# Four x loads on two queues, a split wq, q before k, more dummy matmuls, and wo last: a change to the start and the end of a TensorE-bound attention and feed-forward kernel

## The chip, the cores and the metric

The kernel runs on one core of one Trainium2 chip. The metric is the device time of one execution in microseconds (us). A profiled execution gives a trace; its span, from the first to the last instruction, is 1.5 to 1.8 us shorter than that time.

Engine names are those of the profile: PE is TensorE's matmuls and PEld its weight loads, DVE is VectorE, ACT ScalarE, POOL GpSimd. SP only issues DMA loads and stores; ACT issues some as well ("SPq", "ACTq").

## The reference, cut to what matters

```python
x = A_x                                            # [1, 2048, 512], bf16
g = sigmoid((x * gate_w).sum(-1, keepdims=True))
a = A_ref(x, wq, wk, wv, wo, beta)                 # 32 heads of 16, four segments of 512 tokens
b = B_ref(x, W_gate, W_up, W_down)                 # (relu(x Wg) * (x Wu)) Wd, width 1792
return g * a + (1 - g) * b

# in A_ref, per segment s:
#   a_dot = causal softmax attention within the segment
#   a_mem = phi(q) M / (phi(q) z)                  # memory of the earlier segments
#   o     = sigmoid(beta) * a_mem + (1 - sigmoid(beta)) * a_dot,  then M, z are updated
# the result of A_ref is o @ wo
```

`beta` is 32 numbers, 64 bytes.

Of the kernel before, what the change touches and what calls it, by code (L numbers as in the profile page):

```python
# [18 lines left out]
def mm(n, k=1):  # L19
    return k * (max(n, 60) / 2.4 + 2.5)  # L20
# [359 lines left out]
def program(sc, nc, T, PL, PA, A_x, A_wq, A_wk, A_wv, A_wo, A_beta, W_g, W_u, W_d, gate_w, out, NSEG, KT, NF, NT, EPS, SCALE):  # L380
    V = type("V", (), T)
# [30 lines left out]
    def load(eng, names, dst, src, nbytes, occ=460.0):  # L412
        (lact if eng == "act" else lsp).append(dma(eng, lambda e, dst=dst, src=src: e.dma_start(dst, src), nbytes, occ=occ, writes=names, name="ld" + names[0]))
    x0 = A_x[0, 0:512, :].rearrange("(i p) d -> p i d", p=128)
    for i in (0, 2):
        load("sp", [f"hT{i}", f"hT{i + 1}"], V.hT[:, i:i + 2, :], x0[:, i:i + 2, :], 1 << 18)
    for nm, w, src in (("wq", V.wq, A_wq), ("wk", V.wk, A_wk), ("wv", V.wv, A_wv)):
        load("sp", [nm], w[:], src.rearrange("(kt p) n -> p kt n", p=128), 1 << 19)
    wgr = W_g.rearrange("(kt p) n -> p kt n", p=128)
    wur = W_u.rearrange("(kt p) n -> p kt n", p=128)  # L420
    half = (NF // 2) * 128
# [7 lines left out]
    def load_x(c):  # L429
        for kt in range(KT):  # L430
            lsp.append(dma("sp", lambda e, c=c, kt=kt: e.dma_start_transpose(V.xT[:, kt, c * 512:(c + 1) * 512], A_x[0, c * 512:(c + 1) * 512, kt * 128:(kt + 1) * 128]),
                           1 << 17, occ=1280.0, writes=[f"xT{c}_{kt}"], name=f"ldx{c}_{kt}"))
    load("act", ["braw"], V.braw[:], A_beta.partition_broadcast(128), 8192)
    load_gu(0)
    gsrc = gate_w.rearrange("(kt p) -> p kt", p=128)

# [50 lines left out]
            return ins  # L487
        return pe(fn, n * 427, reads=["rl0"], writes=[f"bankL{b}"], name=f"warm{k}")

    xps, xcs = [warm(5, 0, 3)], []  # L490
    for i in range(4):
        def fx(e, i=i):
            for kt in range(KT):
# [3 lines left out]
        for h in range(2):  # L497
# [3 lines left out]
                xcs.append(dve(lambda e, d=dst, s_=srcp: e.tensor_copy(d, s_), t_dve(256), reads=[f"bankL{i}"], writes=[f"xT0_{i}a"], name=f"xc{i}"))  # L501
            else:
                xcs.append(act(lambda e, d=dst, s_=srcp: e.activation(d, s_, ACT.Copy), t_act(256), reads=[f"bankL{i}"], writes=[f"xT0_{i}b"], name=f"xc{i}"))
    xps.append(warm(2, 1, 0))
    sc.queue(0, xps)
    sc.queue(0, [t for t in xcs if t.eng == "dve"])
    sc.queue(0, [t for t in xcs if t.eng == "act"])
# [49 lines left out]
    def proj(s):  # L557
        pes, evs, sbs, acts, sps = [], [], [], [], []
        tok = s * 512

        def pj(w, col, name, wname, tokmajor=False):
            ep = Epoch("proj")

            for k0 in range(0, KT, 2):
                def fn(e, k0=k0):
                    for kt in (k0, k0 + 1):
                        if tokmajor:
                            ins = e.matmul(A(ep)[:, :], lhsT=V.xT[:, kt, tok + col * 128:tok + (col + 1) * 128], rhs=w[:, kt, :], start=(kt == 0), stop=(kt == KT - 1))  # L568
                        else:
                            ins = e.matmul(A(ep)[:, :], lhsT=w[:, kt, col * 128:(col + 1) * 128], rhs=V.xT[:, kt, tok:tok + 512], start=(kt == 0), stop=(kt == KT - 1))  # L570
                    return ins
                pes.append(pe(fn, mm(512, 2), reads=[wname] + xt(s), name=f"{name}{s}_{col}", ep=ep, role="w2" if k0 else "w"))
            return ep
        for G in range(4):
            ep = pj(V.wq, G, "q", "wq")
            qs = qslot(s, G)
            evs.append(dve(lambda e, ep=ep, qs=qs: e.tensor_copy(V.qT[:, qs, :], A(ep)[:, :]), t_dve(512), writes=[f"qT{qs}"], name=f"qcp{s}_{G}", ep=ep, role="r"))
            if s > 0:
                acts.append(act(lambda e, qs=qs, G=G: e.activation(V.phiq[:, G, :], V.qT[:, qs, :], ACT.Exp), t_act(512, False), reads=[f"qT{qs}"], writes=[f"phiq{G}"], name=f"qexp{s}_{G}"))
                sbs.append(dve(lambda e, qs=qs, G=G: e.tensor_scalar(V.ttmp[:, G % 2, :], V.qT[:, qs, :], 0.0, 1.0, ALU.max, ALU.add), t_dve(512, 4), reads=[f"qT{qs}"], writes=[f"ttmp{G % 2}"], name=f"qts{s}_{G}"))  # L580
                sbs.append(dve(lambda e, G=G: e.tensor_tensor(V.phiq[:, G, :], V.phiq[:, G, :], V.ttmp[:, G % 2, :], ALU.min), t_dve(512, 2), reads=[f"phiq{G}", f"ttmp{G % 2}"], writes=[f"phiq{G}"], name=f"qphi{s}_{G}"))
            ep = pj(V.wk, G, "k", "wk")
            evs.append(dve(lambda e, ep=ep, G=G: e.tensor_copy(V.kT[:, G, :], A(ep)[:, :]), t_dve(512), writes=[f"kT{G}"], name=f"kcp{s}_{G}", ep=ep, role="r"))
            for p in range(2):
                ks = kslot(s, 2 * G + p)
                evs.append(dve(lambda e, G=G, p=p, ks=ks: e.tensor_scalar(V.kp[:, ks, :], V.kT[:, G, :], V.pm[:, p:p + 1], None, ALU.mult), 417, reads=[f"kT{G}", "pm"], writes=[f"kp{ks}"], name=f"kmask{s}_{G}_{p}"))
            if s < NSEG - 1:
                acts.append(act(lambda e, G=G: e.activation(V.ek[:, G, :], V.kT[:, G, :], ACT.Exp), t_act(512, False), reads=[f"kT{G}"], writes=[f"ek{G}"], name=f"kexp{s}_{G}"))
                sbs.append(dve(lambda e, G=G: e.tensor_scalar(V.ttmp[:, G % 2, :], V.kT[:, G, :], 0.0, 1.0, ALU.max, ALU.add), t_dve(512, 4), reads=[f"kT{G}"], writes=[f"ttmp{G % 2}"], name=f"kts{s}_{G}"))
                sbs.append(dve(lambda e, G=G: e.tensor_tensor(V.ek[:, G, :], V.ek[:, G, :], V.ttmp[:, G % 2, :], ALU.min), t_dve(512, 2), reads=[f"ek{G}", f"ttmp{G % 2}"], writes=[f"ek{G}"], name=f"kphi{s}_{G}"))  # L590
                sps.append(dma("sp", lambda e, G=G: e.dma_start_transpose(V.phik[:, :, G * 128:(G + 1) * 128], V.ek[:, G, :]), 1 << 17, occ=1280.0, reads=[f"ek{G}"], writes=[f"phik{G}"], name=f"kT2{s}_{G}"))
        for tt in range(4):
            ep = pj(V.wv, tt, "v", "wv", True)
            evs.append(dve(lambda e, ep=ep, tt=tt: e.tensor_copy(V.vaug[:, s % 2, tt, :, 0:16], A(ep)[:, :].rearrange("q (h c) -> q h c", c=16)), t_dve(512), writes=[f"va{s % 2}_{tt}"], name=f"vcp{s}_{tt}", ep=ep, role="r"))
        return pes, evs, sbs, acts, sps

    def va(s):
# [149 lines left out]
    def outp(s, slots):  # L747
        tiles, evs, sps = [], [], []
        o0 = (s % 2) * 4
        for i in range(4):  # L750
            t = 4 * s + i
            for c0, c1 in (((0, 512),) if t < NT - 1 else ((0, 256), (256, 512))):
                pes = []
                ep = Epoch("out")
                w = c1 - c0

                def fa(e, i=i, ep=ep, c0=c0, c1=c1):
                    for G in range(4):
                        ins = e.matmul(A(ep)[:, 0:c1 - c0], lhsT=V.oT[:, o0 + G, i * 128:(i + 1) * 128], rhs=V.wo[:, G, c0:c1], start=(G == 0), stop=False)  # L759
                    return ins  # L760
                need = slots if s < NSEG - 1 else slots[:NF - 4]
                pes.append(pe(fa, mm(w, 4), reads=[f"oT{o0 + G}" for G in range(4)] + ["wo", "wd"] + [f"hT{x}" for x in need], name=f"oa{s}_{i}", ep=ep, role="w"))
                for f0 in range(0, NF, 2):
                    fs = list(range(f0, min(f0 + 2, NF)))

                    def fb(e, i=i, ep=ep, fs=fs, c0=c0, c1=c1):
                        for f in fs:
                            ins = e.matmul(A(ep)[:, 0:c1 - c0], lhsT=V.hT[:, slots[f], i * 128:(i + 1) * 128], rhs=V.wd[:, f, c0:c1], start=False, stop=(f == NF - 1))  # L768
                        return ins
                    pes.append(pe(fb, mm(w, len(fs)), reads=[f"hT{slots[f]}" for f in fs] + ["wd"], name=f"ob{s}_{i}_{f0}", ep=ep, role="w2"))  # L770
                tiles.append(pes)
                r = t % 3
                om = V.omg[:, t:t + 1]
                res = [f"osb{r}_0", f"osb{r}_1"] if w == 512 else [f"osb{r}_{c0 // 256}"]
                evs.append(sc.add(Op([("dve", lambda e, ep=ep, r=r, om=om, c0=c0, c1=c1: e.tensor_scalar(V.osb[:, r, c0:c1], A(ep)[:, 0:c1 - c0], om, None, ALU.mult), t_dve(w)),  # L775
                                      ("act", lambda e, ep=ep, r=r, om=om, c0=c0, c1=c1: e.activation(V.osb[:, r, c0:c1], A(ep)[:, 0:c1 - c0], ACT.Copy, scale=om), t_act(w, True, 1))],  # L776
                                     reads=[f"omg{min(s, 1)}"], writes=res, name=f"fin{s}_{i}", ep=ep, role="r")))
                sps.append(dma("sp", lambda e, r=r, t=t, c0=c0, c1=c1: e.dma_start(out[0, t * 128:(t + 1) * 128, c0:c1], V.osb[:, r, c0:c1]), w * 256,
                               reads=res, writes=[f"out{t}_{c0}"], name=f"st{t}"))
        if s == NSEG - 1:  # L780
            tiles = [tiles[0][:-1] + tiles[1][:-1] + tiles[0][-1:] + tiles[1][-1:]] + tiles[2:]
        return [p for g in tiles for p in g], evs, sps

    Q = {k: [] for k in ("patt", "pnd", "pmu", "pproj", "pffn", "pout", "exp", "aphi", "dproj", "dsb", "datt", "dnd", "dmu", "effn", "eout", "pool", "poolmu", "spk", "spa", "spo")}
# [32 lines left out]
    sc.queue(1, Q["datt"])  # L817
    for px in ("qcp", "kcp", "vcp"):
        sc.queue(0, [t for t in Q["dproj"] if t.name.startswith(px)])
    sc.queue(1, [t for t in Q["dproj"] if t.name.startswith("kmask")])  # L820
    sc.queue(1, Q["effn"])
    sc.queue(1, Q["eout"])
    sc.queue(1, Q["dnd"])
# [48 lines left out]
```

## The kernel before: the parts that the change and the argument touch

A small list scheduler orders all operations at build time with its own cost model, assigns PSUM banks (where TensorE's results go) and semaphores (counters that tell an engine that something it waits for is done), and emits one program for each engine. So moving one load can reorder the whole program. The loads at the start are these:

```python
x0 = A_x[0, 0:512, :].rearrange("(i p) d -> p i d", p=128)
for i in (0, 2):                                   # two loads of 256 KB, on SP
    load("sp", [f"hT{i}", f"hT{i + 1}"], V.hT[:, i:i + 2, :], x0[:, i:i + 2, :], 1 << 18)
for nm, w, src in (("wq", V.wq, A_wq), ("wk", V.wk, A_wk), ("wv", V.wv, A_wv)):
    load("sp", [nm], w[:], src.rearrange("(kt p) n -> p kt n", p=128), 1 << 19)
# ... cut ...
load("act", ["braw"], V.braw[:], A_beta.partition_broadcast(128), 8192)   # beta to all 128 partitions
load_gu(0)                                         # first halves of W_gate and W_up, on SP
```

The first 512 tokens of x are transposed on TensorE, with dummy matmuls around them that only keep TensorE busy:

```python
xps, xcs = [warm(5, 0, 3)], []                     # five dummy matmuls of 512 columns
for i in range(4):                                 # four 128 x 128 transposes for each x tile
    # ... fx: e.matmul(PL[:, i, ...], lhsT=V.hT[:, i, ...], rhs=V.ident[:]) ...
    # then half of each tile is copied to xT by DVE, the other half by ACT
xps.append(warm(2, 1, 0))                          # two dummies, then the q projections
```

In each segment the projections go q, k, q, k, and so on, then v. In each output tile the four `wo` products come first and 14 `W_down` products follow; the last segment's tiles end the program.

The softmax here doesn't subtract the row's maximum and nothing guards it: scores larger than these inputs give would overflow.

## Time and profile before

| | before |
|---|---|
| time, median of the 6 runs beside the changed kernel | 277.94 us (277.82 to 278.92) |
| span of the profiled execution | 276.13 us |
| PE busy | 269.6 us (98%) |
| first transpose of x | 5.71 us |
| wq landed (issue 1.83 + 6.07) | 7.90 us |
| first weight load of the q projections | 8.54 us |
| end of the last weight load | 273.31 us |

From the page of the profile: span, busy times of the engines, and the chain that ended last, by engine.

```profile
span 276.1 us, 5357 instructions
...
PE 269.6 (98%) x2201; PEld 116.8 (42%) x2201; DVE 196.6 (71%) x390; ACT 193.4 (70%) x171; POOL 91.7 (33%) x152
...
PE 94%; DMA 2%; ACT 2%; DVE 1%; issue 0%
```

TensorE is the limit. A change can help only by starting its stream of useful matmuls sooner, by making that stream shorter, or by ending sooner after it. The start is in the timeline (start, duration, engine, line and operation, count, and in brackets the idle time before it and what ended it):

```profile
0.80 0.42 ACTq L413 DMA_DIRECT2D braw<-in_A_beta_dram  x1
0.80 0.97 SPq L413 DMA_DIRECT2D hT<-in_A_x_dram  x2
...
1.25 2.31 PE L486 MATMUL psL<-rl 128*128 128x512 bf16 x5 [1.25 <-DVE rl L477]
...
5.71 1.89 PE L494 MATMUL psL<-ident,hT 128*128 128x128 bf16 x16 [2.15 <-DMA hT<-in_A_x_dram]
...
7.39 1.06 PE L486 MATMUL psL<-rl 128*128 128x512 bf16 x2
...
8.54 0.13 PEld L570 LDWEIGHTS psA<-xT,wq 128*128 128x128 bf16 x2 [1.00 <-ACT xT L503]
8.55 1.54 PE L570 MATMUL psA<-xT,wq 128*128 128x512 bf16 x4
```

TensorE idles 2.15 us until x lands. The five dummies start 0.43 us apart, twice the 0.215 us that 512-column matmuls take later: the clock is halved. It is still halved for the first q matmuls. The first five matmuls of the projections start at 8.55, 8.95, 9.37, 9.70 and 9.92 us, 1.37 us for four steps that take 0.86 us at the full clock, so 0.51 us of useful work is lost to the clock.

The view of windows gives busy times of PE, PEld, DVE, ACT and POOL in each stretch, then the granted clock (not reliable before the first clock record, as here), the DMA share and the DMA rate in GB/s:

```profile
2.50:3.25 0.75, 0.75 (x3) 0.15 (x1) 0.70 (x2) 0.03 (x1) 0.61 (x3) 1.00 0.50 101
3.25:4.00 0.75, 0.32 (x1) 0.00 (x0) 0.22 (x2) 0.00 (x0) 0.68 (x3) 1.00 0.75 197
...
5.50:6.25 0.75, 0.54 (x6) 0.54 (x7) 0.66 (x6) 0.00 (x0) 0.00 (x0) 1.00 1.03 367
```

The rate takes until after 5 us to pass 300 GB/s. I read this as the ramp of one queue. The timeline of the end:

```profile
271.80 1.52 PEld L768 LDWEIGHTS psA<-wd,hT 128*128 128x128 bf16 x14
271.90 1.69 PE L768 MATMUL psA<-wd,hT 128*128 128x256 bf16 x14
273.63 0.47 ACT L776 ACTIVATE osb<-psA,omg 128x256 bf16<-128x256 f32 x1 [1.43 <-PE psA L768]
```

### The profile page before, as it was taken

To read this page: it belongs to the slowest core of one execution; us is meant where nothing else is said; L and a number is where in the kernel's file an instruction comes from. 1 tells how busy PE (TensorE), PEld (TensorE's weight loads), DVE (VectorE), ACT (ScalarE), POOL (GpSimd) and SP (SyncE) were. 2 spreads that over 40 slices of the span, in tenths; PEclk is the share of its full clock that TensorE was granted. 3 is DMA by queue.
4 is the path that set the end of the run, shared out by engine and by line. 5 is a ranking of instruction groups with operands and counts; after the bars stand their busy time and mean duration, and the time that the engine had idled before them with its cause. 6 is when DMAs were issued, how large, how long until landed. Compare 5 with 4: busy or idle time off the path is not lost.

```text
span 276.1 us, 5357 instructions
## 1 busy us (share of the span) xinstructions
PE 269.6 (98%) x2201; PEld 116.8 (42%) x2201; DVE 196.6 (71%) x390; ACT 193.4 (70%) x171; POOL 91.7 (33%) x152
## 2 busy tenths in 40 slices
PE   5999999999999999999999999999999999999996
PEld 2343444544454434443344444444443444344445
DVE  5789988999897999687989873387766254956210
ACT  2498897798687968776679777775877776753102
POOL 4033332443334534624224333332334333420000
PEclk9999999999999999999999999999999999999999
DMA  5999723100212222000011000000110010000011
GB/s 171 363 258 367 178 56 77 23 2 20 21 20 58 59 57 40 21 19 0 2 38 40 1 21 19 21 19 2 38 38 2 23 37 19 2 0 1 2 38 39
DMA packets 29304, 15.29 MB, mean 55 GB/s; under 512 B 20704, under 2 KB 29280, under 8 KB 29280
## 3 DMA queue, kind: packets, MB, share of 16 engines
q1 hardware_dynamic: 28608, 14.95, 20.8%
q8 instruction: 17, 0.28, 0.4%
q10 hardware_dynamic: 672, 0.01, 0.1%
q14 instruction: 7, 0.06, 0.1%
HBM read 8.14 MB, written 2.10 MB: 37 GB/s over the span
## 4 chain that ended last, share of the span: by engine, by line
PE 94%; DMA 2%; ACT 2%; DVE 1%; issue 0%
PE psA L733 36%; PE psA L768 17%; PE psA L570 11%; PE psL L663 10%; PE psA L688 7%; PE psA L759 5%; PE psA L568 5%; DMA hT<-in_A_x_dram 2%; ACT E L668 1%; PE psA L609 1%; PE psA L638 1%; DVE xT L501 1%; PE psA L526 1%; DVE hT L744 0%; PE psL L494 0%; DVE amem L642 0%
## 5 line engine op out<-in xcount | busy, mean ns | idle before, releaser
L668 ACT ACTIVATE E<-psL 128x2048 bf16<-128x2048 f32 x80 | 150.0, 1875 | 37.0 <-PE psL L663 36.5
L671 POOL TENSOR_SCALAR_AFFINE_SELECT E<-E 128x512 bf16<-128x512 bf16 x128 | 81.8, 656 | 151.4 <-ACT E L668 151.4
L733 PE MATMUL psA<-xT,wg 128*128 128x512 bf16 x224 | 59.5, 380 | 0.0
L733 PE MATMUL psA<-xT,wu 128*128 128x512 bf16 x224 | 59.0, 380 | 0.0
L768 PE MATMUL psA<-wd,hT 128*128 128x512 bf16 (+1 forms) x238 | 55.1, 367 | 0.0
L744 DVE TENSOR_TENSOR hT<-psA,rl 128x512 bf16<-128x512 f32 x56 | 38.2, 683 | 12.3 <-PE psA L733 11.7
L693 DVE STREAM_TRANSPOSE Tn<-psA 128x512 f32<-128x512 f32 x32 | 21.4, 698 | 15.9 <-PE psA L688 15.7
L663 PE MATMUL psL<-qT,kp 32*128 32x384 bf16 (+3 forms) x512 | 31.7, 301 | 0.3 <-ACT E L668 0.3
L768 PEld LDWEIGHTS psA<-wd,hT 128*128 128x128 bf16 x238 | 21.6, 98 | 22.9 <-issue 3.5
L733 PEld LDWEIGHTS psA<-xT,wu 128*128 128x128 bf16 x224 | 20.5, 98 | 25.3 <-issue 2.7
L741 ACT ACTIVATE rl<-psA 128x512 bf16<-128x512 f32 x33 | 19.7, 596 | 16.3 <-PE psA L733 13.8
L733 PEld LDWEIGHTS psA<-xT,wg 128*128 128x128 bf16 x224 | 20.0, 98 | 25.3 <-issue 3.5
L663 PEld LDWEIGHTS psL<-qT,kp 32*128 32x128 bf16 x512 | 8.9, 92 | 31.8 <-ACT E L668 18.7
L688 PE MATMUL psA<-E,vaug 128*17 128x256 bf16 (+3 forms) x512 | 21.1, 300 | 0.1
L775 DVE TENSOR_SCALAR osb<-psA,omg 128x512 bf16<-128x512 f32 x6 | 4.5, 751 | 21.6 <-PE psA L768 21.6
L776 ACT ACTIVATE osb<-psA,omg 128x512 bf16<-128x512 f32 (+1 forms) x11 | 7.1, 648 | 16.1 <-PE psA L768 16.1
L742 DVE TENSOR_SCALAR rl<-psA 128x512 bf16<-128x512 f32 x23 | 15.8, 689 | 3.3 <-PE psA L733 2.8
L570 PE MATMUL psA<-xT,wq 128*128 128x512 bf16 x64 | 17.3, 390 | 0.1
L759 PE MATMUL psA<-wo,oT 128*128 128x512 bf16 (+1 forms) x68 | 16.7, 367 | 0.2 <-DVE amem L642 0.2
L570 PE MATMUL psA<-xT,wk 128*128 128x512 bf16 x64 | 16.8, 380 | 0.0
L568 PE MATMUL psA<-wv,xT 128*128 128x512 bf16 x64 | 15.3, 380 | 0.0
L688 PEld LDWEIGHTS psA<-E,vaug 128*17 128x17 bf16 x512 | 10.5, 90 | 11.2 <-issue 3.4
(68 smaller groups left out, 216.2 us busy)
## 6 DMA issues: line engine op xcount, KB each, us to landing
out_dram<-osb SPq DMA_DIRECT2D x15, 128.0 KB, 1.7
wg<-in_B_W_gate_dram SPq DMA_DIRECT2D x2, 896.0 KB, 7.8
wu<-in_B_W_up_dram SPq DMA_DIRECT2D x2, 896.0 KB, 9.5
wd<-in_B_W_down_dram SPq DMA_DIRECT2D x1, 1792.0 KB, 13.8
hT<-in_A_x_dram SPq DMA_DIRECT2D x2, 256.0 KB, 5.0
wq<-in_A_wq_dram SPq DMA_DIRECT2D x1, 512.0 KB, 6.1
wk<-in_A_wk_dram SPq DMA_DIRECT2D x1, 512.0 KB, 7.1
wv<-in_A_wv_dram SPq DMA_DIRECT2D x1, 512.0 KB, 8.0
```

The costliest lines, as they stand in the source:

```text
L568: ins = e.matmul(A(ep)[:, :], lhsT=V.xT[:, kt, tok + col * 128:tok + (col + 1) * 128], rhs=w[:, kt, :], start=(kt == 0), stop=(kt == KT - 1))
L570: ins = e.matmul(A(ep)[:, :], lhsT=w[:, kt, col * 128:(col + 1) * 128], rhs=V.xT[:, kt, tok:tok + 512], start=(kt == 0), stop=(kt == KT - 1))
L663: ins = q.matmul(PL[:, jj, o:o + w], lhsT=V.kp[32 * jj:32 * jj + 32, kslot(s, n), 128 * j:128 * j + 128], rhs=V.qT[32 * jj:32 * jj + 32, q ...
L668: acts.append(act(lambda a, e=e: a.activation(V.E[:, e, :, :], PL[:, :, :], ACT.Exp, scale=SCALE), t_act(2048), reads=[f"bankL{b}" for b i ...
L671: pools.append(pool(lambda g, ap=ap: g.affine_select(out=ap, in_=ap, compare_op=ALU.is_ge, fill=0.0, base=0, pattern=[[0, 4], [1, 128]], c ...
L688: ins = q.matmul(A(ep)[32 * jj:32 * jj + 17, c:512], lhsT=V.vaug[:, s % 2, j, 8 * G + 2 * jj + p, :], rhs=V.E[:, e, jj, o:o + w], start=(j ...
L693: ds.append(dve(lambda e, p=p, ep=eps[p]: e.transpose(V.Tn[:, p, :], A(ep)[:, :]), t_dve(512), writes=[f"Tn{p}"], name=f"tr{s}_{G}_{p}", e ...
L733: ins = e.matmul(A(ep)[:, :], lhsT=w[:, kt, f * 128:(f + 1) * 128], rhs=V.xT[:, kt, c * 512:(c + 1) * 512], start=(kt == 0), stop=(kt == K ...
L741: evs.append(sc.add(Op([("act", lambda e, ep=eg, r=r: e.activation(V.rl[:, r, :], A(ep)[:, :], ACT.Relu), t_act(512)), ("dve", lambda e, e ...
L744: evs.append(dve(lambda e, ep=eu, r=r, hs=hs: e.tensor_tensor(V.hT[:, hs, :], A(ep)[:, :], V.rl[:, r, :], ALU.mult), t_dve(512), reads=[f" ...
L759: ins = e.matmul(A(ep)[:, 0:c1 - c0], lhsT=V.oT[:, o0 + G, i * 128:(i + 1) * 128], rhs=V.wo[:, G, c0:c1], start=(G == 0), stop=False)
L768: ins = e.matmul(A(ep)[:, 0:c1 - c0], lhsT=V.hT[:, slots[f], i * 128:(i + 1) * 128], rhs=V.wd[:, f, c0:c1], start=False, stop=(f == NF - 1))
```

## The change

The intent is to bring x and wq in sooner by using two DMA queues, to keep TensorE busy so that its clock is full when real work starts, to start with what needs only wq, and to let the last tiles wait as late as possible for the attention's output.

```diff
-    for i in (0, 2):
-        load("sp", [f"hT{i}", f"hT{i + 1}"], V.hT[:, i:i + 2, :], x0[:, i:i + 2, :], 1 << 18)
-    for nm, w, src in (("wq", V.wq, A_wq), ("wk", V.wk, A_wk), ("wv", V.wv, A_wv)):
-        load("sp", [nm], w[:], src.rearrange("(kt p) n -> p kt n", p=128), 1 << 19)
+    for i, eng in enumerate(("sp", "act", "sp", "act")):
+        load(eng, [f"hT{i}"], V.hT[:, i, :], x0[:, i, :], 1 << 17)
+    halves = {}
+    for nm, w, src, cut, engs in (("wq", V.wq, A_wq, 3, ("sp", "act")), ("wk", V.wk, A_wk, 2, ("act", "sp")), ("wv", V.wv, A_wv, 2, ("act", "sp"))):
+        r = src.rearrange("(kt p) n -> p kt n", p=128)
+        for h, (k0, k1) in enumerate(((0, cut), (cut, KT))):
+            load(engs[h], [f"{nm}{h}"], w[:, k0:k1, :], r[:, k0:k1, :], (k1 - k0) << 17)
+            for kt in range(k0, k1):
+                halves[nm, kt] = f"{nm}{h}"
@@
-    load("act", ["braw"], V.braw[:], A_beta.partition_broadcast(128), 8192)
+    load("sp", ["braw"], V.braw[:], A_beta.partition_broadcast(128), 8192)
@@
-    xps, xcs = [warm(5, 0, 3)], []
+    xps, xcs = [warm(6, 0, 3)], []
@@
-    xps.append(warm(2, 1, 0))
+    xps.append(warm(4, 1, 0))
@@ in proj(s)
+        if s == 0:
+            pes = [p for k in "qkv" for p in pes if p.name[0] == k]
@@ in outp(s, slots): cut; per tile the order of the products becomes
+                last = s == NSEG - 1
+                order = ["d"] * (NF // 2) + ["o"] if last else ["o"] + ["d"] * (NF // 2)
@@ DVE's queues: the first two k masks get the highest priority
-    sc.queue(1, [t for t in Q["dproj"] if t.name.startswith("kmask")])
+    km = [t for t in Q["dproj"] if t.name.startswith("kmask")]
+    sc.queue(0, km[:2])
+    sc.queue(1, km[2:])
```

The line about `braw`, the load of beta, looks like tidying: ScalarE's queue is now used for x.

More of the change, by code (lines that the diff above doesn't have):

```diff
@@ L571, in fn @@
                     return ins
-                pes.append(pe(fn, mm(512, 2), reads=[wname] + xt(s), name=f"{name}{s}_{col}", ep=ep, role="w2" if k0 else "w"))
+                pes.append(pe(fn, mm(512, 2), reads=sorted({halves[wname, k0], halves[wname, k0 + 1]}) + xt(s), name=f"{name}{s}_{col}", ep=ep, role="w2" if k0 else "w"))
             return ep
@@ L755, in outp @@
                 w = c1 - c0
-                def fa(e, i=i, ep=ep, c0=c0, c1=c1):
-                    for G in range(4):
-                        ins = e.matmul(A(ep)[:, 0:c1 - c0], lhsT=V.oT[:, o0 + G, i * 128:(i + 1) * 128], rhs=V.wo[:, G, c0:c1], start=(G == 0), stop=False)
-                    return ins
-                need = slots if s < NSEG - 1 else slots[:NF - 4]
-                pes.append(pe(fa, mm(w, 4), reads=[f"oT{o0 + G}" for G in range(4)] + ["wo", "wd"] + [f"hT{x}" for x in need], name=f"oa{s}_{i}", ep=ep, role="w"))
@@ L763, in outp @@
-                for f0 in range(0, NF, 2):
-                    fs = list(range(f0, min(f0 + 2, NF)))
-                    def fb(e, i=i, ep=ep, fs=fs, c0=c0, c1=c1):
-                        for f in fs:
-                            ins = e.matmul(A(ep)[:, 0:c1 - c0], lhsT=V.hT[:, slots[f], i * 128:(i + 1) * 128], rhs=V.wd[:, f, c0:c1], start=False, stop=(f == NF - 1))
-                        return ins
-                    pes.append(pe(fb, mm(w, len(fs)), reads=[f"hT{slots[f]}" for f in fs] + ["wd"], name=f"ob{s}_{i}_{f0}", ep=ep, role="w2"))
+                last = s == NSEG - 1
@@ new lines, in outp, with fa, fb @@
+                order = ["d"] * (NF // 2) + ["o"] if last else ["o"] + ["d"] * (NF // 2)
+                f0 = 0
+                for ci, kind in enumerate(order):
+                    st_, sp_ = ci == 0, ci == len(order) - 1
+                    if kind == "o":
+                        def fa(e, i=i, ep=ep, c0=c0, c1=c1, st_=st_, sp_=sp_):
+                            for G in range(4):
+                                ins = e.matmul(A(ep)[:, 0:c1 - c0], lhsT=V.oT[:, o0 + G, i * 128:(i + 1) * 128], rhs=V.wo[:, G, c0:c1], start=st_ and G == 0, stop=sp_ and G == 3)
+                            return ins
+                        rd = [f"oT{o0 + G}" for G in range(4)] + ["wo"] + ([] if last else ["wd"] + [f"hT{x}" for x in slots])
+                        pes.append(pe(fa, mm(w, 4), reads=rd, name=f"oa{s}_{i}", ep=ep, role="w" if st_ else "w2"))
+                    else:
+                        def fb(e, i=i, ep=ep, f0=f0, c0=c0, c1=c1, st_=st_, sp_=sp_):
+                            for f in (f0, f0 + 1):
+                                ins = e.matmul(A(ep)[:, 0:c1 - c0], lhsT=V.hT[:, slots[f], i * 128:(i + 1) * 128], rhs=V.wd[:, f, c0:c1], start=st_ and f == f0, stop=sp_ and f == f0 + 1)
+                            return ins
+                        rd = [f"hT{slots[f]}" for f in ((f0, f0 + 1) if not st_ else range(NF - 4))]
+                        pes.append(pe(fb, mm(w, 2), reads=rd + ["wd"], name=f"ob{s}_{i}_{f0}", ep=ep, role="w" if st_ else "w2"))
+                        f0 += 2
@@ L780, in outp @@
         if s == NSEG - 1:
-            tiles = [tiles[0][:-1] + tiles[1][:-1] + tiles[0][-1:] + tiles[1][-1:]] + tiles[2:]
+            tiles = [tiles[0][:-2] + tiles[1][:-2] + tiles[0][-2:-1] + tiles[1][-2:-1] + tiles[0][-1:] + tiles[1][-1:]] + tiles[2:]
         return [p for g in tiles for p in g], evs, sps
```

## The prediction

> **What bounds the kernel.** TensorE. The page has PE busy 269.6 of 276.1 us (98%), and the chain of waits that ended last is 94% PE. The view of waits gives PE only about 4 us of waiting, 2.1 of them for x. The timeline splits the span: a head up to 8.55 us, where the first q projection starts; one unbroken stream of matmuls from there to 273.6 us (265 us); a tail of 2.5 us (last eviction, last store). So only head, cold clock and tail can give anything.
>
> **The head now.** Dummies run 1.25 to 3.56 us, PE idles to 5.71 us for x (4.9 us from issue to landing), 16 transposes take 1.6 us, two dummies 1.06 us, and q starts at 8.55 us, just after the last ScalarE copy of xT ends (8.49). wq had landed at 7.93 us (1.83 + 6.1). The clock is still halved: early 512-column matmuls are 0.43 us apart, from about 9.6 us 0.215 us. That costs about 0.5 us of real work.
>
> **What the change does.**
> - x on two queues: the same bytes. The windows of 0.25 to 0.5 us show one queue ramping slowly (about 100 GB/s from 2.5 to 3.25 us, 294 by 4.5, 380 after 6). Two queues should ramp faster: I estimate x 0.3 to 0.5 us earlier (transposes from about 5.3 us). Afterwards nothing is gained: 380 GB/s is the ceiling here. The Trainium skill ("DMA: Bandwidth & Descriptors", "Issuing engines are not separate DMA queues") says that a second issuer saves only issue time; SP's issues cost 0.46 us here.
> - wq: its 3/4 on SP competes with wk's half on ACT, so about 1.28 MB instead of 1.0 MB come before it; at 375 GB/s that is 0.7 us later, less the faster ramp: landing 8.0 to 8.5 us.
> - Dummies: one more in the x wait, free; two more before q, up to 0.43 us each, filling what x gains. So q starts at 8.3 to 8.7 us, hardly earlier, but nearer to the full clock. The skill ("TensorE: Matmul & The Clock Gate", "Part 1: The HAM clock gate") has the clock released after a busy, free-running window of about 3.4 us; the trace agrees roughly (5.71 to 9.6 us). Gain: 0.2 to 0.5 us.
> - q before k: the same 32 projections. The first exp moves from 13.05 to about 16 us. ScalarE (70% busy) isn't the limit, and after the last attention matmul there are still 11.3 us of gate/up matmuls, so this costs nothing.
> - braw goes to SP behind 1.15 MB and lands at about 11 us instead of 5.0; VectorE's third q eviction waits for what depends on it, with some 2 us of slack before PE needs that bank.
> - wo last in the last segment: PE shows no stall between 246.7 and 273.6 us, so 0.
> - The reordered stream has the same 182 runs of one matmul kind in program order, so the same switching cost.
>
> **Sum.** About -0.6 us: 277.35 us, 8 in 10 between 276.6 and 278.1. Faster by over 2%: 1%; within 2%: 98%; slower: 1%.
>
> **What would show it.** Timeline: transposes start near 5.3 us, q at 8.3 to 8.7 us, with 0.215 us spacing from its first or third matmul; quad 0 near 15.5 us; no PE gap until the end; stream still 264 to 265 us; tail 2.5 us.
>
> **What would make it wrong.** The free-running clock window (in the runs before, one of three is 1 us longer) outweighing all of it; wq landing after 9 us; braw stalling VectorE until PE waits for a bank; or the longer wait for the first exp starving PE around 20 us.

## More of the kernel before

At the very end SP waits for all 16 DMA semaphores in turn:

```python
for i in range(sc.ndma):
    if sc.cnt[f"dma{i}"]:
        sc.prog["sp"].append(("wait", f"dma{i}", 16 * sc.cnt[f"dma{i}"]))
```

## The result, and the profile after

| | before | after |
|---|---|---|
| time, median of 6 runs | 277.94 us | 277.12 us (276.17 to 277.94) |
| ratio to before, 95% interval | | 0.9961 (0.9938 to 0.9985) |
| span of the profiled execution | 276.13 us | 275.46 us |
| first transpose of x on PE | 5.71 us | 3.79 us |
| wq landed | 7.90 us | 7.76 us (1.73 + 6.03) |
| first weight load of q | 8.54 us | 7.87 us |
| end of the last weight load | 273.31 us | 272.34 us |
| from there to the end of the span | 2.82 us | 3.11 us |

The result counts as the same within 2%, but the interval excludes 1: it is 0.4% faster.

The span fell by 0.67 us. From the trace: q starts 0.68 us earlier; the cold clock at q's start, 0.51 us, is gone; the rest of the stream is 0.22 us longer (264.48 against 264.77 us in all, where 0.51 us less was due); the tail is 0.30 us longer. The sum is -0.67 us. The page:

```profile
span 275.5 us, 5331 instructions
...
PE 264.6 (96%) x2168; PEld 116.3 (42%) x2204; DVE 199.1 (72%) x391; ACT 191.3 (69%) x170; POOL 92.4 (34%) x152
...
PE 88%; DVE 4%; ACT 2%; DMA 2%; issue 2%; SPq 0%
```

The fall of PE busy to 96% is mostly an artefact: 36 of 2204 matmul records are missing, while all weight loads are there. That is why times of weight loads are used above. The timeline of the start:

```profile
0.80 0.87 SPq L413 DMA_DIRECT2D hT<-in_A_x_dram  x2
0.80 0.90 ACTq L413 DMA_DIRECT2D hT<-in_A_x_dram  x2
...
1.26 2.74 PE L491 MATMUL psL<-rl 128*128 128x512 bf16 x6 [1.26 <-DVE rl L482]
...
3.24 0.47 SPq L413 DMA_DIRECT2D braw<-in_A_beta_dram  x1
...
3.79 1.40 PE L499 MATMUL psL<-ident,hT 128*128 128x128 bf16 x16
...
5.36 1.04 PE L491 MATMUL psL<-rl 128*128 128x512 bf16 x4 [0.17 <-ACT xT L508]
...
7.90 3.61 PE L575 MATMUL psA<-xT,wq 128*128 128x512 bf16 x16 [1.50 <-DMA wq<-in_A_wq_dram]
```

x came some 2 us earlier, not 0.3 to 0.5: its first tile landed at 3.43 us instead of 5.67, its last at 4.21 instead of 6.39. (The first transpose starts only at 3.79 us because the sixth dummy, begun at 3.36 us, runs until then.) TensorE was then busy almost without a break from 1.26 us, and the clock rose inside the transposes: the 16 took 1.40 us instead of 1.89, and the four dummies took 1.04 us, as long as two did before. That is this one execution: in the traces of last_wait, qk_mixed and wo_first, which start with the same loads and dummies, the clock switches at 6.7 to 7.2 us and the four dummies run 0.43 us apart. Then TensorE waited 1.50 us for wq. The windows:

```profile
2.50:3.25 0.75, 0.75 (x3) 0.30 (x2) 0.69 (x2) 0.00 (x0) 0.61 (x3) 1.00 1.01 352
...
9.00:10.00 1.00, 1.00 (x6) 0.46 (x5) 0.83 (x2) 0.00 (x0) 0.00 (x0) 1.00 0.49 164
10.00:11.00 1.00, 1.00 (x6) 0.48 (x5) 0.51 (x1) 0.23 (x1) 0.00 (x0) 1.00 0.98 358
```

At 2.50 us the rate is 352 GB/s where it had been 101. And there is a new hole, 164 GB/s from 9 to 10 us. The raw DMA records show what was in flight there: beta's 128 packets of 64 bytes, from 8.06 to 10.40 us. In the kernel before they were in flight from 1.83 to 4.66 us, just when x crawled. That raised a theory which the prediction did not have.

The end, in the timeline and in SP's raw records (start in us / duration in ns; the last entries are the closing waits, and some wait for two semaphores):

```profile
271.92 0.42 PEld L772 LDWEIGHTS psA<-wo,oT 128*128 128x128 bf16 x4
272.03 0.60 PE L772 MATMUL psA<-wo,oT 128*128 128x256 bf16 x4
272.66 0.47 ACT L789 ACTIVATE osb<-psA,omg 128x256 bf16<-128x256 f32 x1 [1.44 <-PE psA L772]
```

```
before: store issued 274.134; waits 274.518/17 274.576/28 274.649/28 274.713/28 274.775/28 274.834/28 274.896/28 274.955/737
after:  store issued 273.163; waits 273.547/17 273.605/28 273.678/1041 274.755/28 274.817/28 274.876/28 274.938/28 274.997/28
```

The store took about as long in both. But before, the wait that held SP was the last of eight; after, it was the third, and five more followed at 0.06 us each. The new numbering of semaphores costs 0.3 us, as last_wait will show.

### The profile page after: what moved, and what is told of

The parts are those of the page before. It is cut to its first block, busy times and chain, and to the rows that moved or that the text cites. A ratio compares the mean times of both kernels' runs of the same rounds, so it can differ in the third digit from the quotient of the medians.

```text
span 275.5 us, 5331 instructions
## 1 busy us (share of the span) xinstructions
PE 264.6 (96%) x2168; PEld 116.3 (42%) x2204; DVE 199.1 (72%) x391; ACT 191.3 (69%) x170; POOL 92.4 (34%) x152
## 4 chain that ended last, share of the span: by engine, by line
PE 88%; DVE 4%; ACT 2%; DMA 2%; issue 2%; SPq 0%
PE psA L740 35%; PE psA L779 17%; PE psL L670 9%; PE psA L575 9%; PE psA L695 7%; PE psA L772 5%; PE psA L573 5%; DMA wq<-in_A_wq_dram 2%; ACT E L675 2%; PE psA L645 1%; PE psA L616 1%; DVE hT L751 1%; DVE kp L591 1%; DVE qT L582 0%; DVE adT L707 0%
## 5 line engine op out<-in xcount | busy, mean ns | idle before, releaser
L678 POOL TENSOR_SCALAR_AFFINE_SELECT E<-E 128x512 bf16<-128x512 bf16 x128 | 82.8, 664 | 148.4 <-ACT E L675 145.6
L740 PE MATMUL psA<-xT,wg 128*128 128x512 bf16 x215 | 57.6, 380 | 1.4 <-issue 1.3
L740 PE MATMUL psA<-xT,wu 128*128 128x512 bf16 x217 | 57.7, 380 | 0.8 <-issue 0.6
L779 PE MATMUL psA<-wd,hT 128*128 128x512 bf16 (+1 forms) x228 | 53.5, 367 | 1.1 <-issue 0.8
L748 ACT ACTIVATE rl<-psA 128x512 bf16<-128x512 f32 x29 | 17.2, 597 | 13.9 <-PE psA L740 11.3
L749 DVE TENSOR_SCALAR rl<-psA 128x512 bf16<-128x512 f32 x27 | 18.4, 683 | 4.4 <-PE psA L740 3.7
L575 PE MATMUL psA<-xT,wq 128*128 128x512 bf16 x60 | 16.1, 380 | 2.0 <-DMA wq<-in_A_wq_dram 1.5
L789 ACT ACTIVATE osb<-psA,omg 128x512 bf16<-128x512 f32 (+1 forms) x10 | 6.4, 644 | 15.6 <-PE psA L772 13.3
L772 PE MATMUL psA<-wo,oT 128*128 128x512 bf16 (+1 forms) x65 | 15.8, 366 | 0.4 <-issue 0.3
L582 DVE CAST qT<-psA 128x512 bf16<-128x512 f32 x16 | 10.9, 683 | 4.0 <-PE psA L575 3.9
```

What stands on the lines that cost most here:

```text
L575: ins = e.matmul(A(ep)[:, :], lhsT=w[:, kt, col * 128:(col + 1) * 128], rhs=V.xT[:, kt, tok:tok + 512], start=(kt == 0), stop=(kt == KT - 1))
L678: pools.append(pool(lambda g, ap=ap: g.affine_select(out=ap, in_=ap, compare_op=ALU.is_ge, fill=0.0, base=0, pattern=[[0, 4], [1, 128]], c ...
L740: ins = e.matmul(A(ep)[:, :], lhsT=w[:, kt, f * 128:(f + 1) * 128], rhs=V.xT[:, kt, c * 512:(c + 1) * 512], start=(kt == 0), stop=(kt == K ...
L749: ("dve", lambda e, ep=eg, r=r: e.tensor_scalar(V.rl[:, r, :], A(ep)[:, :], 0.0, None, ALU.max), t_dve(512))],
L772: ins = e.matmul(A(ep)[:, 0:c1 - c0], lhsT=V.oT[:, o0 + G, i * 128:(i + 1) * 128], rhs=V.wo[:, G, c0:c1], start=st_ and G == 0, stop=sp_ a ...
L779: ins = e.matmul(A(ep)[:, 0:c1 - c0], lhsT=V.hT[:, slots[f], i * 128:(i + 1) * 128], rhs=V.wd[:, f, c0:c1], start=st_ and f == f0, stop=sp ...
```

## The experiments

Theories at the start: **S**, a load of a single 128-row tile starts delivering sooner; **Q**, the second queue does it; **D0/D1**, the added dummies do nothing, or keep the clock. **B**, that the small beta load beside x is what slows x, came after the first runs. Every kernel gave the reference's result. The before-kernels of the same rounds had medians of 277.73 to 277.96 us.

| run | time, median (range), us | ratio to before (95%) | first weight load of a transpose | of q |
|---|---|---|---|---|
| after | 277.12 (276.17-277.94) | 0.9961 (0.9938-0.9985) | 3.47 | 7.87 |
| x4_oneq | 279.33 (277.76-279.50) | 1.0030 (1.0004-1.0056) | 3.75 | 8.52 |
| x2_twoq | 280.75 (280.01-281.62) | 1.0104 (1.0083-1.0124) | 4.16 | 10.39 |
| x4_twoq | 279.37 (278.55-280.75) | 1.0059 (1.0032-1.0087) | 3.62 | 8.36 |
| wq_four | 276.63 (276.36-276.89) | 0.9952 (0.9937-0.9968) | 3.48 | 6.78 |
| few_dummies | 277.12 (276.24-277.61) | 0.9961 (0.9934-0.9989) | 3.52 | 8.31 |
| qk_mixed | 277.81 (276.86-279.89) | 0.9998 (0.9960-1.0035) | 3.61 | 8.68 |
| wo_first | 277.36 (276.00-279.70) | 0.9974 (0.9928-1.0020) | 3.55 | 8.90 |
| last_wait | 276.42 (275.79-279.27) | 0.9951 (0.9911-0.9991) | 3.71 | 7.57 |
| braw_late | 280.32 (278.38-280.87) | 1.0065 (1.0035-1.0095) | 3.70 | 7.50 |
| braw_first | 276.50 (276.46-278.31) | 0.9957 (0.9933-0.9982) | 3.94 | 7.72 |
| wq_four_last | 276.21 (275.54-276.91) | 0.9936 (0.9917-0.9955) | 3.36 | 6.51 |
| one_queue | 276.32 (275.84-276.81) | 0.9941 (0.9922-0.9959) | 3.77 | 7.74 |

Much of the scatter is the clock. The slowest execution of last_wait (279.27 us), of qk_mixed (279.89) and of wo_first (279.70), and four of the six of braw_late, have a mean granted clock of 0.993 or 0.994; the others of these runs have 0.999 or 1.000. One stretch of 3.41 us at half clock would give such a mean (estimate: 1 - 0.5 x 3.41 / 278 = 0.994) and cost 1.7 us of matmuls; braw_late's trace shows one.

### x4_oneq: before, with x in four loads on one queue

```diff
-    for i in (0, 2):
-        load("sp", [f"hT{i}", f"hT{i + 1}"], V.hT[:, i:i + 2, :], x0[:, i:i + 2, :], 1 << 18)
+    for i in range(4):
+        load("sp", [f"hT{i}"], V.hT[:, i, :], x0[:, i, :], 1 << 17)
```

> The kernel before, with one edit: x's first four tiles come in four loads of 128 KB, all on SP's queue; all else as before. Theory S (shape: a load of one 128-row tile starts delivering sooner than a load of two tiles): the first transposes start by 4.0 us instead of 5.71, the DMA rate passes 250 GB/s by 2.75 us, the clock is full before the first q projection, and the time is 0.5 to 1.0 us below before (about 277.1 us). Theory Q (the second queue does it): the rate ramps as before, about 100 GB/s until 3.25 us, transposes not before 5.0 us, time within 0.3 us of before.

The first tile was early (3.75 us), the rate was between S and Q (161 GB/s from 2.50 to 3.25 us), and the last tile landed only at 5.91 us (6.39 before). So with beta still beside x, smaller loads bring the first tile early, but hardly the last. The time rose, which neither theory had: four executions took 279.3 to 279.5 us and two 277.8 to 277.9, no longer than before; the traced one is of the four. TensorE idled 0.7 us before the last tile and 1.13 us for wq, and the trace's clock record shows full speed only from 12.54 us: some ten matmuls of q and k ran 0.43 us apart. An early first tile is worth nothing if the clock is still halved when the work starts.

### x2_twoq: before, with the two whole x loads on two queues

```diff
-    for i in (0, 2):
-        load("sp", [f"hT{i}", f"hT{i + 1}"], V.hT[:, i:i + 2, :], x0[:, i:i + 2, :], 1 << 18)
+    for i, eng in ((0, "sp"), (2, "act")):
+        load(eng, [f"hT{i}", f"hT{i + 1}"], V.hT[:, i:i + 2, :], x0[:, i:i + 2, :], 1 << 18)
```

> The kernel before, with one edit: the two 256 KB x loads stay whole, but one goes to ScalarE's queue. Theory S: both still start slowly, first transposes at 5.2 us or later, time within 0.4 us of before. Theory Q: the rate passes 250 GB/s by 2.75 us, transposes start by 4.2 us, time 0.5 to 1.0 us below before.

Transposes started at 4.16 us, which speaks against S alone. The time rose by 1%, and the timeline of ACT shows why:

```profile
1.32 0.52 ACTq L413 DMA_DIRECT2D braw<-in_A_beta_dram  x1
1.86 1.28 ACT L509 ACT_TABLE_LOAD   x1 [1.86 <-issue]
7.91 0.23 ACT L509 ACTIVATE eb<-braw 128x32 f32<-128x32 bf16 x1 [4.77 <-DMA braw<-in_A_beta_dram]
...
9.41 0.94 ACT L503 ACTIVATE xT<-psL 128x256 bf16<-128x256 f32 x3
```

Beta now stood behind x on ScalarE's queue. The scheduler had placed the exponential of beta ahead of the copies of xT, so ScalarE sat 4.77 us on it, with the copies behind it, while x was ready. While beta's packets were in flight (4.11 to 7.51 us) the whole DMA rate was 187 GB/s, just before it 369 and just after it 364. This pattern gave theory B.

### x4_twoq: before, with the x part of the change alone

```diff
-    for i in (0, 2):
-        load("sp", [f"hT{i}", f"hT{i + 1}"], V.hT[:, i:i + 2, :], x0[:, i:i + 2, :], 1 << 18)
+    for i, eng in enumerate(("sp", "act", "sp", "act")):
+        load(eng, [f"hT{i}"], V.hT[:, i, :], x0[:, i, :], 1 << 17)
```

> The kernel before, with the x part of the change alone: four loads of one tile each on two queues. Both theories: transposes from about 3.8 us, PE waits for wq afterwards, which lands at 7.4 to 8.0 us, q starts there at the full clock; time 0.6 to 1.1 us below before, so that this part alone is the whole gain. If it gains under 0.3 us, the rest of the change is needed for it.

Transposes came at 3.62 us as expected, but the time rose by 0.6%: again ScalarE waited for beta (3.48 us, until 6.99), and q, k and the next q ran with 0.43 us between matmuls, at half clock. The part that names the change is, alone, a loss.

### wq_four: the changed kernel with wq in four loads

```diff
+        if nm == "wq":
+            for kt in range(KT):
+                load(("sp", "act")[kt % 2], [f"wq{kt}"], w[:, kt, :], r[:, kt, :], 1 << 17)
+                halves[nm, kt] = f"wq{kt}"
+            continue
```

> The changed kernel, with wq in four loads of one 128-row slice each, alternately on the two queues, instead of three slices on SP and one on ScalarE. Theory S: these start delivering at once too, the dip of the DMA rate at 3.5 to 4.5 us goes away, wq lands by 6.4 us instead of 7.76, q starts at 6.4 to 6.7 us, and the time falls by 1.0 to 1.5 us below the changed kernel (about 275.8 us). Rival (bytes and queue share limit wq, not its shape): wq lands no earlier than 7.3 us and the time falls by under 0.4 us.

q's first weight load came at 6.78 us, 1.09 us earlier, as wq landed at 6.68, so wq's arrival had been the limit. The time fell by 0.5 us only (277.12 to 276.63). The first q matmul started at 7.18 us, not 6.78: the four dummies ran at half clock until the switch at 7.15 us, and the last of them held it. So here the added dummies cost some 0.4 us. And the tail grew again, to 2.71 us from the issue of the last store: its semaphore now fell first in the closing waits, with seven more behind it (0.45 us), and the program's closing steps after the waits took 0.2 us more than in the changed kernel, which is not explained. The dip of the DMA rate after x stayed (111 to 209 GB/s from 3.75 to 4.75 us), so theory S did not explain that either.

### few_dummies, qk_mixed, wo_first: the changed kernel with one part undone each

```diff
few_dummies:  warm(6, 0, 3) -> warm(5, 0, 3);  warm(4, 1, 0) -> warm(2, 1, 0)
qk_mixed:
-        if s == 0:
-            pes = [p for k in "qkv" for p in pes if p.name[0] == k]
wo_first:
-                last = s == NSEG - 1
+                last = False
```

(wo_first also restores before's list of what the first product of a tile waits for, and its order of the first two tiles.)

> The changed kernel with the dummy matmuls as before (five and two instead of six and four). Theory D0 (the added dummies do nothing): PE is busy without a gap over 0.5 us from 1.25 us to the end of the transposes anyway, the clock is full by about 4.5 us, q still starts when wq lands (about 7.9 us), time within 0.2 us of the changed kernel. Theory D1 (they keep the clock): early 512-column matmuls of q are 0.43 us apart and the time rises by 0.3 to 0.8 us.

> The changed kernel with q and k projections alternating as before. Theory: wk lands at about 9.2 us, so the first k projection, due at about 8.75 us, waits 0.3 to 0.5 us on TensorE, and the time rises by 0.2 to 0.5 us although the first exp comes some 2 us earlier. Rival (an early exp is worth more): the time falls by 0.3 us or more.

> The changed kernel with the wo products first in each tile of the last segment, as before. Theory: nothing waits in the last 27 us either way, time within 0.2 us of the changed kernel apart from which final semaphore wait comes last (up to 0.3 us in the tail). Rival: wo last is worth over 0.3 us in TensorE's stream, seen as waits of PE between 245 and 273 us.

few_dummies equals the changed kernel to 0.01 us in the median; q ran at the full clock from its first matmul, the switch having come at 6.69 us. The added dummies gained nothing that these runs can see. qk_mixed and wo_first have medians 0.7 and 0.2 us higher, but the ranges and the intervals overlap with the changed kernel's, so the times settle neither part's effect. The traces say more. From q's first weight load to the end of the last weight load the stream took 264.48 us in the changed kernel and in few_dummies, 264.40 in qk_mixed and 264.47 in wo_first: none of the three parts changes it by more than 0.1 us. In qk_mixed the expected wait for wk did not show: the second half of wk landed at 9.95 us, and the first k matmuls started at 9.57, 9.78, 10.00 and 10.23 us, at the usual step. But q itself had started 0.8 us late there; with q at 7.9 us the wait might have come. Its tail was 0.37 us longer than the changed kernel's, all of it after the closing waits. In wo_first PE shows no wait near the end.

These runs and last_wait share the changed kernel's load plan, yet wq landed at 7.46 (last_wait), 7.76 (the changed kernel), 8.21, 8.57 and 8.80 us in their profiles, and q started 0.1 us later in each. So wq's landing varies from one execution to the next by more than most parts of the change are worth. I put the rest of their wide ranges, beside the three executions at a lower clock, down to that, though only one execution of each was traced.

### last_wait: the changed kernel with the closing waits in the order of the stores

```diff
-    for i in range(sc.ndma):
+    for i in sorted(range(sc.ndma), key=lambda i: sc.dma_end.get(i, 0.0)):
```

> The changed kernel with SP's closing waits sorted so that the semaphore of the store issued last is waited for last. In the changed kernel five more waits of about 0.06 us each follow its landing; in the kernel before none did. Theory: the time from the issue of the last store to the end of the span falls from 2.3 to 2.0 us, total 0.2 to 0.4 us less. Rival (the store itself landed late): no change.

From the issue of the last store to the end: 1.99 us, against 2.29 in the changed kernel and 2.00 before. The holding wait came last again. The median fell by 0.7 us, of which 0.3 us is this. In the traced execution another 0.3 us is q's earlier start (7.57 instead of 7.87 us); for the other executions that is not shown, and the intervals overlap.

### braw_late: before, with only the beta load moved

```diff
-    load("act", ["braw"], V.braw[:], A_beta.partition_broadcast(128), 8192)
+    load("sp", ["braw"], V.braw[:], A_beta.partition_broadcast(128), 8192)
```

> The kernel before, with one edit: the 8 KB broadcast load of beta goes to SP's queue behind wv instead of ScalarE's queue beside x. [...] Theory B (this small load is a large part of what made x slow in the kernel before): the two whole 256 KB loads of x alone on SP pass 250 GB/s by 3.25 us and the first transposes start by 4.7 us instead of 5.71. Theory S/Q (only shape or queues matter): transposes start at 5.4 us or later. The time may still not fall, since then TensorE idles until wq and its clock is half again: 277.3 to 279 us.

Windows, with x in two whole loads on SP alone:

```profile
2.50:3.25 0.75, 0.75 (x3) 0.15 (x1) 0.69 (x2) 0.00 (x0) 0.61 (x3) 1.00 1.05 366
3.25:4.00 0.75, 0.62 (x5) 0.30 (x5) 0.22 (x2) 0.00 (x0) 0.68 (x3) 1.00 1.03 315
```

366 GB/s instead of 101, and transposes from 3.70 us instead of 5.71. Theory B holds: moving 8 KB gives 2.0 us of the change's 2.2 us in x's landing, with one queue and two loads. x landed 2.9 to 3.0 us after issue instead of 4.9 to 5.1.

The time nevertheless rose by 2.4 us in the median, above the expected range. Four executions took 280.1 to 280.9 us at a mean clock of 0.993 or 0.994, two 278.4 and 278.6 at 1.000; the traced one is of the four. Windows around the switches of the clock that the trace records at 5.55, 8.96 and 12.38 us:

```profile
5.60:8.90 3.30, 1.49 (x6) 0.32 (x4) 0.76 (x3) 0.78 (x3) 0.00 (x0) 1.00 0.97 325
9.00:12.30 3.30, 3.30 (x8) 1.07 (x9) 1.06 (x3) 0.86 (x2) 0.00 (x0) 0.50 0.89 315
```

TensorE waited 1.46 us for wq and 0.37 us for wk, was busy in less than half of that stretch, and lost its clock just as the work began: 3.4 us at half speed, about 1.7 us of work lost. Besides, the first exp of the attention came at 22.43 us instead of 13.05, because the scheduler had put VectorE's first k mask at 20.92 us, behind copies that need beta (the change gives the first two masks priority); the attention then ended late (its last matmul at 254.6 us instead of 246.5), and the first `wo` product waited 1.74 us for it near 258 us. The switches are 3.41 and 3.42 us apart. That fits the Trainium skill, "TensorE: Matmul & The Clock Gate", "Part 1: The HAM clock gate", which gives a free-running window of 3413 ns.

### braw_first: the changed kernel with the beta load ahead of x

```diff
+    load("act", ["braw"], V.braw[:], A_beta.partition_broadcast(128), 8192)
     x0 = A_x[0, 0:512, :].rearrange("(i p) d -> p i d", p=128)
@@
-    load("sp", ["braw"], V.braw[:], A_beta.partition_broadcast(128), 8192)
```

> The changed kernel with the broadcast load of beta issued first on ScalarE's queue, as in the kernel before, ahead of x. Theory B: the DMA rate stays under 250 GB/s from 1.75 to 3.5 us, the first transposes start 0.5 to 1.5 us later (4.0 to 5.0 us), wq lands at 8.3 us or later and the time rises by 0.5 us or more. Theory S/Q: transposes still by 3.9 us, time within 0.3 us of the changed kernel.

```profile
2.50:3.25 0.75, 0.75 (x3) 0.29 (x2) 0.69 (x2) 0.00 (x0) 0.61 (x3) 1.00 0.75 117
3.25:4.00 0.75, 0.75 (x3) 0.06 (x2) 0.22 (x2) 0.10 (x1) 0.68 (x3) 1.00 0.79 212
```

The slow ramp is back, with x in four loads on two queues; beta's packets were in flight from 1.99 to 3.67 us. The last transposes started at 6.14 us. So that beta slows x is confirmed from the other side. The time, however, did not rise (276.50 us; the interval overlaps with the changed kernel's): my expectation was wrong on that. The two parts of wq landed at 6.37 and 7.51 us, the later one still before the changed kernel's 7.76, with beta out of the way after 3.7 us; q started at 7.72 us, at the full clock, held by the copies of xT; and the stream that the scheduler built was 0.5 us shorter. Waits of 0.65 us near 85.6 us, 0.55 near 96.1 and 0.61 near 111.5, which stand in the weight loads of the changed kernel, are missing in it. In 13 of the 14 traces all loads together moved at only 140 to 300 GB/s while beta's packets were in flight, wherever it stood. What counts is whether something that TensorE waits for is behind it.

### one_queue: the changed kernel with x, wq, wk and wv whole, on SP alone

```diff
-    for i, eng in enumerate(("sp", "act", "sp", "act")):
-        load(eng, [f"hT{i}"], V.hT[:, i, :], x0[:, i, :], 1 << 17)
+    for i in (0, 2):
+        load("sp", [f"hT{i}", f"hT{i + 1}"], V.hT[:, i:i + 2, :], x0[:, i:i + 2, :], 1 << 18)
 # and one load for each of wq, wk, wv on SP, as before
```

> The changed kernel with all loads of x, wq, wk and wv whole and on SP's queue as in the kernel before (x in two loads of 256 KB, each weight in one), everything else as changed: beta's broadcast behind wv, q before k, six and four dummies, wo last. Theory B (what freed x is where the beta load stands, and neither the second queue nor the smaller loads are needed): first transposes by 4.0 us, wq lands at 7.3 to 8.3 us, q starts there at the full clock, time within 0.4 us of the changed kernel (276.7 to 277.5 us). Rival (the split loads carry the gain): time at or above the kernel before (277.9 us), with q at 8.5 us or later.

```profile
1.26 2.74 PE L489 MATMUL psL<-rl 128*128 128x512 bf16 x6 [1.26 <-DVE rl L480]
3.79 1.91 PE L497 MATMUL psL<-ident,hT 128*128 128x128 bf16 x16
5.50 1.22 PE L489 MATMUL psL<-rl 128*128 128x512 bf16 x4
7.77 3.61 PE L573 MATMUL psA<-xT,wq 128*128 128x512 bf16 x16 [1.05 <-DMA wq<-in_A_wq_dram]
```

276.32 us, below the expected range and at least as fast as the changed kernel, without its named idea. x landed at 3.73 and 4.38 us, 0.2 to 0.3 us after the changed kernel's first and last tile; the transposes still start at the same 3.79 us, as the sixth dummy ends only then. q is within 0.13 us, the stream is equal (264.48 us), and the tail is 0.31 us shorter, as the holding wait came last. Neither the second queue nor the split loads are needed for the gain. This agrees with the Trainium skill, "DMA: Bandwidth & Descriptors", "Issuing engines are not separate DMA queues", by which a second issuer saves only the time of issuing.

But braw_first is as fast with beta's load back in front. one_queue undoes the split, braw_first undoes beta's move, and both start q by 7.8 us at the full clock. So in time either of the two is enough beside the rest of the change; a kernel with both undone was not run, and what the rest alone is worth is open.

### wq_four_last: the version the runs point to

The edits of wq_four and last_wait together.

> The version the runs point to: the changed kernel with wq in four loads of one slice, and the closing waits in order of the stores. wq_four alone started q at 6.78 us, but its tail from the issue of the last store to the end was 2.71 us, as its semaphore fell first in the closing waits. Expected: q at 6.6 to 7.0 us, that tail 2.0 us, time about 275.9 us (275.5 to 276.3), below both kernels.

276.21 us, ratio 0.9936: the fastest median of all, though its interval touches those of one_queue and last_wait. q started at 6.51 us, a little before the expected range, with a step of 0.29 us instead of 0.22 from its second matmul to its third, which waited for the third slice of wq. The clock had switched at 4.61 us, so here the dummies delayed nothing. The tail was 2.29 us, not the expected 2.0; the holding wait was the last, and the closing steps after it took some 0.25 us more than in the changed kernel, which I did not pursue.

## Why the prediction was right or wrong

The time was right: 277.12 us against 277.35, inside the range. The size of the gain was about right too, 0.6 us predicted and 0.8 us measured. Several terms of the sum were not, and that they added up is luck.

- **"TensorE ... only head, cold clock and tail can give anything"**: right. The 0.67 us of the span come from these, less 0.2 us that the reordered stream lost.
- **"I estimate x 0.3 to 0.5 us earlier", because two queues ramp faster**: wrong in cause and size. x came 2.2 us earlier (its last tile from 6.39 to 4.21 us), and braw_late and one_queue show that moving the beta load does it. The trace of before had the clue: the page lists two queues, the second with 672 packets and 0.01 MB (128 of them are beta's, 512 the load of `gate_w`), and beta's packets thin out just where the rate rises. A second clue is the fit in the Trainium skill, "DMA: Bandwidth & Descriptors", "Anatomy of one DMA — SWDGE (gpsimd) path", 2.0 us plus bytes over 436 GB/s. It was measured for another way of issuing, but as an estimate it gives 2.6 us for 256 KB; 4.9 us asked for an explanation, and 2.9 us is what the load takes with beta out of the way.
- **"wq ... landing 8.0 to 8.5 us"**: 7.76 us in the trace, somewhat early; over five traces with this load plan it landed between 7.46 and 8.80 us, so the forecast lies within what the plan gives.
- **"Dummies ... up to 0.43 us each ... q starts at 8.3 to 8.7 us"**: wrong, 7.87 us. With x early TensorE was never idle for long, so the clock was full before the second set of dummies, which ran 0.22 us apart. They ended at 6.4 us and delayed nothing; in few_dummies they were not needed either. That they did not delay q is partly luck: in three traces with the same start they ran 0.43 us apart, as predicted, but wq landed later still, and in wq_four, where wq came early, they held q until 7.18 us.
- **"Nearer to the full clock. Gain: 0.2 to 0.5 us"**: right in size, 0.51 us, but not by the added dummies: in few_dummies q ran at the full clock without them.
- **"q before k ... costs nothing"**: right in that PE did not wait for the later exp (first at 15.40 us, about 16 predicted), and the stream of qk_mixed is equal within 0.1 us.
- **"braw ... lands at about 11 us", with slack**: right, 10.75 us. DVE waited 0.52 us, PE did not. But I listed this as a cost only, and missed that the move is what lets x land 2 us earlier. How much of the 0.8 us in time hangs on it is not shown: braw_first takes it back and is not slower.
- **"wo last ... so 0"**: right; the stream of wo_first is equal to 0.01 us.
- **"tail 2.5 us", unchanged**: wrong by 0.3 us, from the order of the closing waits.

So the head gave 0.68 us of an earlier q, where hardly any was forecast, and a stream 0.22 us longer than due and a tail 0.30 us longer, neither of them forecast, took most of that back. A right total did not mean a right account.

## What to carry to other kernels

When a load lands much later than its size explains, look at everything else in flight at that time before blaming its queue or its shape; a tiny broadcast can cost more than a large tile (here an estimated 0.3 MB of other transfers), so put it behind what the busiest engine is waiting for. An engine whose clock is halved at the start is best kept busy up to the first real work: bringing its data earlier without its next input (x without wq here) made the kernel slower in most executions of x4_oneq and braw_late, because, in the traced ones, the work then ran at half clock (in braw_late a late attention cost time as well). (In x2_twoq and x4_twoq, slower too, ScalarE's wait for beta stood in the way as well.) And undo each part of a compound change alone before crediting the part that gave it its name.

## What the Trainium skill lacked or had wrong

- "DMA: Bandwidth & Descriptors" says that transfers under 64 KB pay mostly overhead, and how queues take turns on a DMA engine, but gives no figure for what such a load does to others beside it. Here a load of 64 bytes broadcast to 128 partitions (8 KB, 128 packets of 64 bytes) was in flight for 1.2 to 3.6 us. In 13 of the 14 traces the rate of all loads meanwhile was 140 to 300 GB/s, in wq_four_last 327; in the ten traces where full-rate loads stood around it (all but before, x4_oneq, x4_twoq and braw_first), the rate was 335 GB/s or more in the microsecond before and after. As an estimate from the changed kernel (2.34 us at 217 GB/s instead of about 355), that is 0.3 MB of lost transfer. Small packets alone are not the reason: the load of `gate_w` puts 512 packets of 2 bytes in flight from 10.04 to 13.54 us of the changed kernel, and the rate meanwhile was 365 GB/s. Why beta's load is so slow is open.
- No page has the cost of closing waits: SP waits for the DMA semaphores one after the other at about 0.06 us each, so that a last store in third place of eight costs 0.3 us (2.29 against 1.99 us), and in first place, in wq_four, 0.45 us (another 0.2 us of its 2.71 come after the waits).
- "TensorE: Matmul & The Clock Gate" gives the window, and asks for no idle gap over about 3 us, but not how much work within a window keeps the clock. In braw_late it was lost with no single wait over 1.46 us. Counted in stretches of 3.41 us before and after each recorded switch, with PE busy as the profile models it, braw_late lost the clock after 1.58 us busy; wo_first kept it with 1.61 us and few_dummies with 1.76 us. Half clock was released after 2.99 us busy in few_dummies, and not after 2.49 us in wq_four. The rule is open.
- No page explains the dip to 138 to 195 GB/s from 4.00 to 4.75 us, right after x, that one_queue and the changed kernel show without beta in flight. few_dummies and last_wait, with the changed kernel's loads, had 304 and 317 GB/s there, so it varies between executions. It stays open.
